# The matrices of the D transform loaded in eight transfers with the half as outer index, a new ranking of the first stage's work list, and the residual rows' first load in halves

## The chip, the cores and the metric

One core of a Trainium2 chip runs the whole program. The metric is the device time of one execution in microseconds, the median of several runs. The engines that matter are PE (TensorE, matmuls), DVE (VectorE), ACT (ScalarE), POOL (GpSimd) and SP (SyncE), which only issues transfers here. Transfers run on the core's 16 DMA engines.

## The reference

A transformer-like block on x of 2048 rows and 512 columns: a layer norm with a modulation from c, a Fourier mixing (a DFT over the 512 columns, then one over the 2048 rows, the real part kept), a residual, a second modulated norm, and a SwiGLU of width 1792. In float32, with tight agreement asked for.

```python
mod = (silu(c) @ w_mod).reshape(c.shape[0], 6, 1, -1)
sa, ca, ga, sb, cb, gb = (mod[:, i] for i in range(6))
h = layernorm(x) * (1 + ca) + sa
a = einsum("bsd,ed->bse", h, dft_hid_re)
b = einsum("bsd,ed->bse", h, dft_hid_im)
y = einsum("ts,bse->bte", dft_seq_re, a) - einsum("ts,bse->bte", dft_seq_im, b)
x = x + ga * y
h = layernorm(x) * (1 + cb) + sb
x = x + gb * ((silu(h @ w1) * (h @ w3)) @ w2)
```

## The kernel before

**Stages.** The first stage makes the D transform (over the 512 columns) of all 2048 rows, the second the sequence transform over the rows, the last the second norm and the SwiGLU. The stages follow each other on PE; transfers and preparations for a later one run beside an earlier one. The symmetry of the DFT matrices is used: rows s and 2048 - s are handled together, as sums and differences, which halves the matmuls. Sums of squares are formed beside the work to confirm that the matrices given have that symmetry; else a general path, which stands behind a branch, would compute all again.

**Precision.** Each float32 operand is split into a high and a low part; a product is three matmuls (high by high, high by low, low by high). ACT makes the high parts by a copy, DVE the low parts by a subtraction. So every matrix and every block passes ACT and DVE before PE can use it.

**The first stage.** The rows come in 8 blocks k of 256 (two sides of 128: a block and its mirror image). For each block: DVE takes the statistics of both sides (`stats`), ACT the root, DVE the inverse; ACT or DVE scale the two sides (`scale`, L468 or L470); PE transposes them (`turn`, L485); ACT or DVE apply the modulation (`mod`, L501 or L503, tile hm); DVE makes sums and differences (`sum`, tile hs); ACT their high parts (`hh`), DVE their low parts (`hl`); ACT also copies the mirror side (`h1`). PE then multiplies by the four D matrices dt = 0 to 3 (`prod`, L559), by their differences (`diff`, L576) and the mirror side (`mirror`, L598). ACT and DVE split the results into us, ul and uh, the operands of the sequence matmuls (L750). For block 4 the mirror part h1 has a low part too (DVE, tile h).

**The D matrices.** `load_hid(dt)` (L226 to L231) fetches one of four matrices into the tile raw_w[dt] (named w in the profile): 128 partitions, real and imaginary part side by side, 512 columns each. Partition q * 64 + r holds half q, row r of 64; in memory the rows r lie 8 KB apart and the two halves q 2 KB apart. Four transfers of 64 rows of 2 KB fetch one matrix. `w_highs` (ACT) and `w_lows` (DVE) split it into the tile wu, `w_minus` (ACT) makes a negated copy wn of the first two, `differ_w` (DVE) the differences wd.

**Order of the loads.** SP issues, in this order: cc, one side of x0, part of w_mod's rows (wmr), w0, w1, x1, w2, w3, x2, x3 and then one side of x4 to x7. ACT issues the other side of x0 and two loads of wmr. POOL fetches the mirrored sides of x4 to x7 by an indirect transfer, each behind a difference wd (`load_x`, L202).

**Order of the work.** After a fixed opening (norm of block 0, the modulation's vectors, some warming matmuls of L281 that keep PE busy), a planner orders the first stage: `task(name, rank, needs, fn, engine = us)` lists a piece of work, `arrange` takes again and again, among the pieces whose needs are met earliest within a window, the one with the lowest rank, and writes it to its engine. Ranks are a base per block (PACE 7.39) plus an entry of the table RANK; assumed arrival times of the loads are given by `at(...)` (L1518 to L1523). The result is one fixed order for each engine, and the engines run it strictly in that order. While the planned PE time has gaps before the first products, the planner fills them with warming matmuls.

**The residual.** `load_xt(t)` (L798) fetches a quarter of the rows of x, transposed, into two tiles; it is issued at step k = 2 (and 5) of a sequence pass, and `residual` first uses it at the end of step 3 (and 7).

Of the kernel before, what the change touches and what calls it, by code (L numbers as in the profile page):

```python
# [42 lines left out]
def folded(nc, pools, c, cp, wmr, wmc, x, xt, ctr, cti, wdr, wdi, w1, w3, w2, out):  # L43
# [15 lines left out]
    def take(dt=F32, what="s"):  # L59
        slot = free.popleft()  # L60
        count[0] += 1
        t = big.tile([P, 2, N], dt, name=f"{what}_{count[0]}", tag=f"slot{slot}")
        slot_of[id(t)] = (slot, t)
        return t
# [85 lines left out]
    mirror = consts.tile([P, NT, 2, NK // 2], I32, name="mirror")  # L150
# [73 lines left out]
    raw_w = {}  # L224

    def load_hid(dt, queue):  # L226
        i, par = HD[dt]
        raw_w[dt] = take(F32, "w")
        for m, w in enumerate((wdr, wdi)):
            for q in range(2):  # L230
                queue.dma_start(raw_w[dt][q * 64 : (q + 1) * 64, m, :], w[i][par::2, q])  # L231

    nc.sync.dma_start(cc, cp)
    load_x(0, nc.scalar)
# [4 lines left out]
    for dt in range(2):  # L239
        load_hid(dt, nc.sync)  # L240
    load_x(1)
    for dt in range(2, ND):
        load_hid(dt, nc.sync)
# [220 lines left out]
    def norm_scale(k, side, engine):  # L464
        r = rs[k][1]
        a, by, add = xz[k][:, side, :], r[:, 0, side : side + 1], r[:, 1, side : side + 1]
        if engine == "ACT":
            nc.scalar.activation(a, a, AF.Identity, bias=add, scale=by)  # L468
        else:
            nc.vector.tensor_scalar(a, a, by, add, op0=OP.mult, op1=OP.add)  # L470


    turned, hm, hs, h1 = {}, {}, {}, {}
    hh, hl = {}, {}
# [19 lines left out]
    def modulate_rows(k, dt, engine):  # L494
        if k not in hm:
            hm[k] = take(F32, "hm")
        src = turned[k][dt // 2][:, (dt % 2) * HALF : (dt % 2 + 1) * HALF]
        dst = four(hm[k])[:, dt, :]
        sa, ca1 = mod1[:, 0, dt : dt + 1], mod1[:, 1, dt : dt + 1]
        if engine == "ACT":  # L500
            nc.scalar.activation(dst, src, AF.Identity, bias=sa, scale=ca1)  # L501
        else:
            nc.vector.tensor_scalar(dst, src, ca1, sa, op0=OP.mult, op1=OP.add)  # L503
# [35 lines left out]
    uh, us, ul = {}, {}, {}  # L539
# [256 lines left out]
    xr = {}  # L796

    def load_xt(t):  # L798
        xr[t] = [take(F32, "xr") for _ in range(2)]
        for i in range(2):  # L800
            nc.sync.dma_start(xr[t][i], xt[t, i])

    def residual(t, e, src, gate):
        xs = xr[t][e // 2][:, e % 2, :]
# [261 lines left out]
    turn = [0, 0]  # L1066
# [393 lines left out]
    def at(us, *names):  # L1460
        for name in names:
            ends[name] = (us, "DMA")

    def last_steps(k):
# [6 lines left out]

    PACE = 7.39
    RANK = {
        "stats": -18.2,
        "root": -47.5,
        "inverse": -47.1,
        "scale": -41.6,
        "turn": -4.3,
        "mod": -3.8,
        "sum": -42.2,  # L1480
        "hh": -19.0,
        "hl": -6.5,
        "h1": -11.0,
        "prod": 2.1,
        "odd": -9.0,
        "mirror": 61.7,
        "uh": 12.4,
        "us": 4.0,
        "ul": 3.9,
        "diff": 21.3,  # L1490
        "up": -6.8,
        "ush": 27.9,
        "ulh": 31.5,
    }
    seq_steps = []
    keep_warm(3)
# [21 lines left out]
    at(10.0, "turn0.0", "turn0.1")  # L1518
    for dt in range(ND):
        at(13.6 + 0.25 * dt, f"modc{dt}")  # L1520
        at((13.4, 15.2, 18.3, 20.3)[dt], f"w{dt}")
    for k in range(1, 4):
        at((16.5, 21.8, 23.3)[k - 1], f"x{k}")  # L1523
    clear.update(PE=14.2, DVE=14.5, ACT=12.2, POOL=9.0, SP=9.0)
    for k in range(4, NK):
        task(f"load{k}", 2 * k - 7, [f"wd{min(k - 4, 2) + 1}"], lambda k=k: load_x(k), POOL=1.0)
# [10 lines left out]
    for k in range(NK):  # L1537
        r = k * PACE
        both = [f"{k}.0", f"{k}.1"]
        if k:  # L1540
# [10 lines left out]
            for s in range(2):  # L1551
                task(
                    f"scale{k}.{s}", r + RANK["scale"] + s, [f"inverse{k}"],
                    lambda e, k=k, s=s: norm_scale(k, s, e), ACT=0.71, DVE=0.46,
# [5 lines left out]
        for dt in range(ND):  # L1560
            task(
                f"mod{k}.{dt}", r + RANK["mod"] + 0.1 * dt, [f"modc{dt}", *[f"turn{n}" for n in both]],
                lambda e, k=k, dt=dt: modulate_rows(k, dt, e), ACT=0.45, DVE=0.46,
# [83 lines left out]
    for n, (j, k) in enumerate(steps):  # L1647
        if k == 2:
            load_xt(j + 2)
        if k == 5:  # L1650
            load_xt(j)
# [884 lines left out]
def fnet_swiglu_block(  # L2536
# [26 lines left out]
    pools = consts, small, big, psum  # L2563
    args = c, cp, wmr, wmc, x, xt, ctr, cti, wdr, wdi, w1, w3, w2, out
    bad = folded(nc, (*pools, dram, tc), *args)
    flag = nc.values_load(
        bad[0:1, 0:1],
# [62 lines left out]
```

## Time and profile before

| | |
|---|---|
| median of 3 runs (lowest, highest) | 692.43 us (691.5, 692.43) |
| the profiled execution: its own time | 691.3 us |
| its span in the profile | 689.5 us |
| granted clock of PE | 0.997 |
| DMA: packets, MB, mean rate | 40262, 116.80 MB, 169 GB/s |
| window 60 to 70 us: PE, DVE, ACT busy | 8.71, 9.48, 8.03 us |

The span begins with the first instruction of the program and ends with the last; the 1.8 us between it and the profiled time lie outside. In the profile's rows, "12.76 0.42 ACT L87 ..." is a start, a duration (both us), the engine, the line of the kernel, the operation and its operands; "[0.99 <-DMA w]" says that the engine was idle 0.99 us before it, and what ended that. A row of a table by windows gives the window, its length, each engine's busy time with its number of instructions, PE's granted clock, the busy share of the 16 DMA engines and the GB/s that they moved. SPq and POOLq are the queues from which these engines issue transfers. Buffer numbers are left out, so w stands for all four raw matrices.

### The profile page before, as it was taken

Reading aid. Unit: us, or ns where it says so; the run is one execution under the profiler, and the core shown is the slowest. Engines: PE = TensorE matmul, PEld = TensorE weight load, DVE = VectorE, ACT = ScalarE, POOL = GpSimd, SP = SyncE. Lnnn points to the kernel's source line nnn. Section 1 sums busy time; section 2 is a strip of 40 time slices with the busy share of each in tenths; the row PEclk is TensorE's granted clock in tenths of the full one; section 3 lists DMA queues with packets and bytes.
Section 4 is the critical chain, followed back from the end, with each engine's and each line's share of the span. In section 5 each row is a group of like instructions: output and inputs, shape, how many; then the busy total and the mean of one; then the engine's idle time right before and its main releaser. Section 6 shows DMA issues by size and latency. Waiting matters only on the chain.

```text
span 689.5 us, 9030 instructions
## 1 busy us (share of the span) xinstructions
PE 673.1 (98%) x3122; PEld 557.5 (81%) x3122; DVE 586.7 (85%) x945; ACT 451.2 (65%) x751; POOL 134.2 (19%) x156
## 2 busy tenths in 40 slices
PE   6999999999999999999999999999999999999996
PEld 4898788888888888888788888887878888888785
DVE  5999769997999977989997989787998979888375
ACT  4998956455343665663577767867677887877520
POOL 1320172544435000100101101011012112221100
PEclk9999999999999999999999999999999999999998
DMA  8730199887678441274757666466939998999813
GB/s 264 222 125 1 52 371 329 261 293 262 190 291 291 153 149 30 51 135 122 134 140 127 150 153 123 96 131 120 277 74 213 162 202 165 180 217 170 182 42 126
DMA packets 40262, 116.80 MB, mean 169 GB/s; under 512 B 5137, under 2 KB 5393, under 8 KB 40209
## 3 DMA queue, kind: packets, MB, share of 16 engines
q0 software_dynamic: 14512, 50.86, 36.8%
q1 hardware_dynamic: 25264, 63.98, 27.9%
q10 hardware_dynamic: 432, 1.31, 0.5%
q8 instruction: 26, 0.43, 0.3%
q14 instruction: 28, 0.22, 0.1%
HBM read 76.81 MB, written 41.42 MB: 171 GB/s over the span
## 4 chain that ended last, share of the span: by engine, by line
PE 75%; issue 8%; DVE 7%; ACT 4%; DMA 4%; POOL 1%; SPq 1%; POOLq 0%; DVEq 0%; ACTq 0%
PE bank L100 45%; PE bank L750 26%; DMA sum<-y 2%; PE bank L559 2%; POOL sum L1352 1%; PE bank L598 1%; DMA w<-in_wdr 1%; SPq L231 1%; DVE xr L805 1%; PE bank L576 1%; DMA x<-in_x 1%; ACT y L335 0%; DVE ul L90 0%; DVE hl L90 0%; ACT hh L87 0%
## 5 line engine op out<-in xcount | busy, mean ns | idle before, releaser
L100 PE MATMUL bank<-hf,w2h 128*128 128x512 f32 (+1 forms) x352 | 108.3, 389 | 0.0
L87 ACT ACTIVATE hf<-v 128x512 fp32r<-128x512 f32 x71 | 44.4, 631 | 67.3 <-DVE v L96 54.4
L335 ACT ACTIVATE y<-bank,gb 128x512 f32<-128x512 f32 x118 | 76.5, 682 | 4.0 <-PE bank L100 3.9
L100 PEld LDWEIGHTS bank<-hf,w2h 128*128 128x128 f32 x352 | 65.6, 188 | 15.3 <-ACT y L335 1.5
L1160 POOL DMA_DIRECT2D sum<-y x28 | 24.0, 857 | 240.7 <-ACT y L335 124.6
L100 PE MATMUL bank<-hf,w2l 128*128 128x512 f32 (+1 forms) x176 | 68.2, 387 | 0.0
L90 DVE TENSOR_TENSOR hf<-v,hf 128x512 fp32r<-128x512 f32 x71 | 48.7, 686 | 10.4 <-ACT hf L87 10.3
L1352 POOL DMA_DIRECT2D sum<-y x35 | 29.8, 852 | 128.8 <-ACT y L335 119.8
L87 ACT ACTIVATE x<-bank 128x512 f32<-128x512 f32 x72 | 41.8, 591 | 13.5 <-PE bank L100 12.6
L750 PE MATMUL bank<-l,us 128*128 128x512 f32 x128 | 49.9, 390 | 0.0
L750 PE MATMUL bank<-d,us 128*128 128x512 f32 x128 | 49.9, 390 | 0.0
L750 PE MATMUL bank<-bh,us 128*128 128x512 f32 x128 | 49.9, 390 | 0.0
L750 PE MATMUL bank<-d,uh 128*128 128x512 f32 x128 | 49.9, 390 | 0.0
L750 PE MATMUL bank<-bh,ul 128*128 128x512 f32 x128 | 49.8, 389 | 0.0
L750 PE MATMUL bank<-l,uh 128*128 128x512 f32 x128 | 49.8, 389 | 0.0
L170 POOL DMA_INDIRECT re<-in_ctr,mirror x32 | 36.3, 1136 | 65.5 <-ACT im L188 40.1
L170 POOL DMA_INDIRECT im<-in_cti,mirror x32 | 34.2, 1069 | 32.5 <-PE bank L750 8.5
L93 DVE TENSOR_TENSOR x<-bank,x 128x512 f32<-128x512 f32 x36 | 24.7, 685 | 17.8 <-PE bank L100 17.8
L100 PEld LDWEIGHTS bank<-hf,w2l 128*128 128x128 f32 x176 | 33.1, 188 | 6.7
L1244 ACT ACTIVATE v<-v 128x512 f32<-128x512 f32 x36 | 22.6, 629 | 23.2 <-DVE v L93 22.8
L93 DVE TENSOR_TENSOR v<-bank,x 128x512 f32<-128x512 f32 x36 | 24.7, 686 | 14.9 <-PE bank L100 14.0
L100 PE MATMUL bank<-h2h,w1h 128*128 128x512 f32 x80 | 31.2, 390 | 0.0
(260 smaller groups left out, 1902.1 us busy)
## 6 DMA issues: line engine op xcount, KB each, us to landing
sum<-y POOLq DMA_DIRECT2D x63, 512.0 KB, 5.5
w<-in_w SPq DMA_DIRECT2D x42, 512.0 KB, 5.0
re<-in_ctr SPq DMA_DIRECT2D x32, 256.0 KB, 5.4
im<-in_cti SPq DMA_DIRECT2D x32, 256.0 KB, 5.2
wmc<-in_wmc SPq DMA_DIRECT2D x8, 512.0 KB, 7.9
xr<-in_xt SPq DMA_DIRECT2D x8, 512.0 KB, 8.0
sum<-xr SPq DMA_DIRECT2D x8, 512.0 KB, 6.3
x<-in_x SPq DMA_DIRECT2D x11, 256.0 KB, 4.6
```

Source lines behind the costliest of these rows:

```text
L87: nc.scalar.activation(dst, src, AF.Copy, scale=scale)
L90: nc.vector.tensor_tensor(out=dst, in0=a, in1=b, op=OP.subtract)
L93: nc.vector.tensor_tensor(out=dst, in0=a, in1=b, op=OP.add)
L100: nc.tensor.matmul(acc, lhs[a], rhs[b], start=first and n == 0, stop=last and n == len(PASSES) - 1, skip_group_check=more,)
L170: nc.gpsimd.indirect_dma_start(dst, None, rows, bass.IndirectOffsetOnAxis(ap=at, axis=0))
L231: queue.dma_start(raw_w[dt][q * 64 : (q + 1) * 64, m, :], w[i][par::2, q])
L335: nc.scalar.activation(dst, src, AF.Identity, scale=by)
L559: nc.tensor.matmul(halves(hb[k])[:, m, :], sides((hh, hl)[a][k])[:, dt, m, :], wu[dt][:, b, m, :], start=False, stop=dt % 2 == 1 and n == ...
L750: nc.tensor.matmul(acc[what, e], lhs, rhs, start=begin and i == 0, stop=(end or (turn and what == "x")) and i == len(terms) - 1, skip_grou ...
L1160: nc.gpsimd.dma_start(sums[t, d // 2], y, accum_op=OP.add)
L1244: behind(k != 0 or q == 0, lambda: nc.scalar.activation(v, src, AF.Silu))
L1352: nc.gpsimd.dma_start(sums[t, which], y, accum_op=OP.add)
```

## The change

Three edits.

```diff
         for m, w in enumerate((wdr, wdi)):
-            for q in range(2):
-                queue.dma_start(raw_w[dt][q * 64 : (q + 1) * 64, m, :], w[i][par::2, q])
+            queue.dma_start(raw_w[dt][:, m, :], w[i][par::2].rearrange("r q n -> q r n"))
...
         xr[t] = [take(F32, "xr") for _ in range(2)]
-        for i in range(2):
-            nc.sync.dma_start(xr[t][i], xt[t, i])
+        for q in range(2):
+            nc.sync.dma_start(xr[t][0][:, q, :], xt[t, 0, :, q])
+        nc.sync.dma_start(xr[t][1], xt[t, 1])
...
     RANK = {
-        "stats": -18.2,
-        "root": -47.5,
...
+        "stats": -18.7,
+        "root": -45.0,
...
     for dt in range(ND):
         at(13.6 + 0.25 * dt, f"modc{dt}")
-        at((13.4, 15.2, 18.3, 20.3)[dt], f"w{dt}")
+        at((12.4, 14.2, 17.2, 18.8)[dt], f"w{dt}")
     for k in range(1, 4):
-        at((16.5, 21.8, 23.3)[k - 1], f"x{k}")
+        at((15.8, 20.6, 22.3)[k - 1], f"x{k}")
```

A part (real or imaginary) of a D matrix is now one transfer of 128 rows of 2 KB, whose source counts the half q outermost (2), then the row r (64). The destination is the same. All twenty entries of RANK and the assumed arrivals of w0 to w3 and x1 to x3 have new values, so that the planner makes another order. The first of the two tiles of each residual load comes in two transfers of 256 KB.

On SP, in the opening, the loads of the first two matrices (w) and of block 1 (x). Before:

```order
L231 DMA w_99<-in_wdr 64x512 x2
L231 DMA w_99<-in_wdi 64x512 x2
L231 DMA w_104<-in_wdr 64x512 x2
L231 DMA w_104<-in_wdi 64x512 x2
L209 DMA x_109<-in_x 128x1x512
```

Now:

```order
L230 DMA w_99<-in_wdr 128x1x512
L230 DMA w_99<-in_wdi 128x1x512
L230 DMA w_102<-in_wdr 128x1x512
L230 DMA w_102<-in_wdi 128x1x512
L209 DMA x_105<-in_x 128x1x512
```

Half the rows, in the same places of the queue; the other two matrices follow x1 in the same way.

On ACT, around the conversion of the last two matrices (wu from w_112 and w_117 before, from w_108 and w_111 now; wn is a negated copy, rs the root of block 1, hh and h parts of block 0, x the scaling of block 1, hm its modulation). Before:

```order
L87 ACTIVATE wn_244<-wu_224 128x1024
L454 ACTIVATE rs_235<-mv_234,eps 128x2
L87 ACTIVATE wu_250<-w_112 128x256 x2
L87 ACTIVATE hh_255<-hs_246 128x4x128
L468 ACTIVATE x_109<-x_109,rs_235 128x512
L87 ACTIVATE wu_294<-w_117 128x256 x2
L87 ACTIVATE hh_255<-hs_246 128x4x128
L87 ACTIVATE h_35_308<-hm_219 128x512
L501 ACTIVATE hm_314<-bank_31_288,mod_147 128x256 x2
```

Now:

```order
L87 ACTIVATE wu_233<-w_108 128x256 x2
L453 ACTIVATE rs_224<-mv_223,eps 128x2
L87 ACTIVATE hh_240<-hs_236 128x4x128
L87 ACTIVATE wu_244<-w_111 128x256 x2
L87 ACTIVATE h_30_273<-hm_211 128x512
L87 ACTIVATE hh_240<-hs_236 128x4x128
L467 ACTIVATE x_105<-x_105,rs_224 128x512
L87 ACTIVATE wn_295<-wu_213 128x1024
L500 ACTIVATE hm_307<-bank_32_289,mod_139 128x256 x2
```

The scaling of x1 and the second negated copy wn have moved from ahead of the last matrix's conversion to behind it.

On DVE, around the scaling of block 5 (x_380 before, x_385 now; hs, h and hl are parts of block 4, ho is the odd half of block 3). Before:

```order
L93 TENSOR_TENSOR hs_627<-hm_597 128x4x128
L90 TENSOR_TENSOR hs_627<-hm_597 128x4x128
L459 RECIPROCAL rs_537<-rs_537 128x2
L460 SCALAR_TENSOR_TENSOR rs_537<-mv_536,rs_537 128x2
L470 TENSOR_SCALAR x_380<-x_380,rs_537 128x512 x2
L93 TENSOR_TENSOR ho_549<-bank_70_508,ho_549 128x512
L90 TENSOR_TENSOR h_90_662<-hm_597,h_90_662 128x512
L90 TENSOR_TENSOR hl_673<-hs_627,hh_646 128x1024
```

Now:

```order
L93 TENSOR_TENSOR hs_627<-hm_591 128x4x128
L90 TENSOR_TENSOR hs_627<-hm_591 128x4x128
L458 RECIPROCAL rs_599<-rs_599 128x2
L459 SCALAR_TENSOR_TENSOR rs_599<-mv_598,rs_599 128x2
L90 TENSOR_TENSOR h_89_648<-hm_591,h_89_648 128x512
L93 TENSOR_TENSOR ho_532<-bank_71_513,ho_532 128x512
L469 TENSOR_SCALAR x_385<-x_385,rs_599 128x512 x2
L90 TENSOR_TENSOR hl_668<-hs_627,hh_652 128x1024
```

The scaling of x5 stands behind h and ho, no longer ahead of them.

More of the change, by code (lines that the diff above doesn't have):

```diff
@@ L1473, in folded @@
     RANK = {
-        "stats": -18.2,
-        "root": -47.5,
[L1476 to L1493, printed above, removed]
+        "stats": -18.7,
+        "root": -45.0,
+        "inverse": -61.3,
+        "scale": -16.6,
+        "turn": -8.5,
+        "mod": -4.5,
+        "sum": -74.2,
+        "hh": -16.7,
+        "hl": -4.4,
+        "h1": -22.1,
+        "prod": 4.2,
+        "odd": -82.1,
+        "mirror": 90.1,
+        "uh": 21.2,
+        "us": 25.0,
+        "ul": 0.6,
+        "diff": 18.2,
+        "up": -0.8,
+        "ush": 21.0,
+        "ulh": 47.4,
     }
```

## The prediction

> **What bounds the kernel now.** I read the page first, then PE's waits in the first stage, then the loads in front of that stage.
>
> ```profile
> span 689.5 us, 9030 instructions
> ...
> PE 673.1 (98%) x3122; PEld 557.5 (81%) x3122; DVE 586.7 (85%) x945; ACT 451.2 (65%) x751; POOL 134.2 (19%) x156
> ...
> PE 75%; issue 8%; DVE 7%; ACT 4%; DMA 4%; POOL 1%; SPq 1%; POOLq 0%; DVEq 0%; ACTq 0%
> ```
>
> PE is busy for 98% of the span, and three quarters of the chain of waits are PE's own work. What the change touches lies before the first sequence matmul. Some of PE's work there is only the warming matmuls of L281, so 98% tells nothing of that part. From the first product on, PE waits like this (waits by engine and line, then the timeline):
>
> ```profile
> PE bank L549 <- DVE ho L93: 1.8, 2, 1.6
> PE bank L598 <- ACT h L87: 1.0, 1, 1.0
> PE bank L559 <- ACT hh L87: 0.4, 1, 0.4
> PE bank L100 <- ACT y L335: 0.5, 1, 0.5
> PE bank L100 <- ACT x L87: 0.4, 1, 0.4
> ...
> 21.87 0.51 PE L559 MATMUL bank<-wu,hh 128*128 128x256 f32 x2 [0.44 <-ACT hh L87]
> ...
> 83.76 0.39 PE L750 MATMUL bank<-bh,us 128*128 128x512 f32 x1
> ```
>
> The first product starts at 21.87 us, the first sequence matmul at 83.76, with 3.2 us of waits between (L549, L598, L559; the two of L100, 0.9 us, belong to the last stage). That 3.2 us is all that a better order behind the loads could return; an earlier start comes on top. What sets 21.87? These rows of ACT and of the matrices' transfers:
>
> ```profile
> 12.76 0.42 ACT L87 ACTIVATE wu<-w 128x256 fp32r<-128x256 f32 x1 [0.99 <-DMA w<-in_wdr]
> ...
> 17.30 1.23 SPq L231 DMA_DIRECT2D w<-in_wdi  x2
> ...
> L231 SPq DMA_DIRECT2D w<-in_wdr x8: 465/596/618, 4.2 to 16.7; - x8
> ...
> 19.45 1.05 ACT L87 ACTIVATE wn<-wu 128x1024 fp32r<-128x1024 f32 x1
> ...
> 21.72 0.81 ACT L468 ACTIVATE x<-x,rs 128x512 f32<-128x512 f32 x1
> 22.43 0.71 ACT L87 ACTIVATE wu<-w 128x256 fp32r<-128x256 f32 x2
> ...
> DMA to landing us min/median/max: 3.5/4.5/7.9
> ```
>
> ACT has all four matrices to convert, in a fixed order. The last piece is issued at 17.9 us (second of the two at 17.30), with the median of 4.5 us it is there at about 22.4, and the conversion of the last matrix (ACT, 22.43) follows at once. From that conversion to the first sequence matmul are 83.76 - 22.43 = 61.33 us. Whatever moves the last matrix moves the whole rest one for one, unless another wait comes first.
>
> **The change part by part.** *The transfers.* The number of bytes is the same, in 8 issues in place of 16. SP saves 8 x 0.6 = 4.8 us of issuing (596 ns each in the row above). What matters is how fast one transfer runs. The rates, by stretch (last two columns: share of the 16 DMA engines, GB/s):
>
> ```profile
> 5.00:10.00 5.00, 3.18 (x12) 1.58 (x11) 2.76 (x8) 2.23 (x5) 0.00 (x0) 1.00 1.03 408
> 10.00:15.00 5.00, 3.91 (x28) 3.04 (x27) 4.24 (x7) 2.60 (x5) 0.00 (x0) 1.00 1.08 256
> 15.00:17.00 2.00, 2.00 (x20) 2.00 (x19) 1.11 (x7) 0.92 (x3) 0.00 (x0) 1.00 0.97 308
> 26.00:28.00 2.00, 2.00 (x15) 1.66 (x13) 1.94 (x4) 2.00 (x4) 1.83 (x2) 1.00 0.97 343
> ```
>
> One busy engine moves 408/16/1.03 = 24.8 GB/s (5 to 10 us, partly rows of 4 KB), 16 (the old w transfers of 64 rows, 10 to 15 us, taken as full), 19.8 and 22.1 (15 to 17 and 26 to 28 us, x rows of 2 KB). All that is with 16 engines. Does the new transfer use 16? Its source now counts 2 (the half), then 64 rows; every transfer of before counts 64 or 128 rows first. How these were shared out can be read off ACT's queue:
>
> ```profile
> q1 hardware_dynamic: 25264, 63.98, 27.9%
> q10 hardware_dynamic: 432, 1.31, 0.5%
> ...
> wmr<-in_wmr ACTq DMA_DIRECT2D x2, 512.0 KB, 6.8
> ...
> x<-in_x ACTq DMA_DIRECT2D x1, 256.0 KB, 3.5
> ```
>
> ACT issued three transfers of 128 rows, 384 packets; the other 48 of the 432 are 16 for each, an end mark from every engine. Rows counted by 64 x 2 (x) and by 128 (wmr) both went to all 16 engines, in equal shares of the outermost count (4 and 8). A share that is a run of the outermost loop is the simplest reading of both; with an outermost count of 2 there are only two shares, and 14 engines stand idle for each of the eight. No row of before has an outermost count under 64, so this is an inference and not a reading.
>
> The Trainium skill speaks to just this: "DMA: Bandwidth & Descriptors", section "Why a DMA increments its semaphore by 16 and not by 1", says that a transfer runs on the largest number of engines, up to 16, that divides the slowest count (other than 1) of both its sides, and its "Rules for kernel authors" warn of an outermost count below 16. By it the number here is 2, and the sum is the one that follows; the transfers of before, with 64 and 128, agree with it, and no run here shows a smaller one.
>
> On two engines each carries half of 8 x 256 KB, 1049 KB. At 24.8 GB/s that takes 42.3 us, at 22.1 47.5, at 16 65.5. I take 23.6 (44.4 us): two engines alone have nobody to contend with, so the two fastest rows are nearest. x1's two halves stand between the matrices in the same queue, with 16 KB each per engine: 1.4 us more. The first: ACT's row at 12.76 starts when the first 256 KB are there, which at 256 GB/s take 1.0 us, so they flow in from about 11.7. The last piece then lands at 11.7 + 44.4 + 1.4 = 57.5 us in place of 22.4.
>
> *The list.* On ACT two rows change sides around the last conversion: x1's scaling and the second negation (wn) stood ahead of it and now stand behind it. Starts in the rows above give their cost: 22.43 - 21.72 = 0.71 and 20.40 - 19.45 = 0.95 (the statistics' root follows at 20.40). Of the last matrix's own two copies the first no longer waits for the second's transfer (-0.3 of the 0.71). So 61.33 + 0.71 + 0.95 - 0.3 = 62.7 us lie behind the landing. Queued on ACT behind this conversion, and so waiting with it, are the copy h of block 0, the high halves hh that PE's products need, and block 1's modulation; DVE's lows and PE wait for those. The rows for this and for DVE's part:
>
> ```profile
> 20.40 0.29 ACT L454 ACTIVATE rs<-mv,eps 128x2 f32<-128x2 f32 x1
> ...
> 47.98 1.00 DVE L470 TENSOR_SCALAR x<-x,rs 128x512 f32<-128x512 f32 x2
> 48.89 0.68 DVE L93 TENSOR_TENSOR ho<-bank,ho 128x512 f32<-128x512 f32 x1
> 49.68 0.69 DVE L90 TENSOR_TENSOR h<-hm,h 128x512 fp32r<-128x512 f32 x1
> ```
>
> On DVE x5's two scalings (47.98) stood ahead of h and ho and now stand behind both, 1.2 to 1.4 us later for PE's transposes; PE's waits of 3.2 us may go in exchange. I enter 0 for this pair, with bounds -3.2 and +1.4.
>
> *x2 to x7* queue behind the last matrix: two 256 KB transfers for x2 add 2 x 0.7 = 1.4 us, so it is there at 58.9. Before, x2 was first used about 2 us behind the last conversion; no further wait. POOL's mirrored x loads follow DVE's differences of these matrices and move with them.
>
> *The residual's first load* in two issues: four more on SP, 0.6 us each, and the same bytes. A load takes
>
> ```profile
> xr<-in_xt SPq DMA_DIRECT2D x8, 512.0 KB, 8.0
> ...
> 83.99 0.39 PE L750 MATMUL bank<-bh,ul 128*128 128x512 f32 x1
> ```
>
> 8.0 us, and is issued two steps ahead of its use. A step has 48 matmuls of L750, 0.23 us apart (83.76 and 83.99 for the first two), so the cover is 22 us: nothing, and with that cover gone 0.6 us each.
>
> **Sum.** First sequence matmul at 57.5 + 62.7 = 120.2, against 83.76: +36.4. Behind it PE has only the 0.9 us of waits at L100, none of them on a load, so all of it arrives at the end. The profiled execution took 691.3 us (span 689.5): 727.7. The median of the runs shown, 692.43, is 1.1 above it: 728.8, so 729.
>
> A sentence aside: the Trainium skill's "TensorE: Matmul & The Clock Gate", section "What's actually happening", has PE fall to half clock after some 3.4 us of idleness and rise after as much work; by that page my estimate is another 1 to 2 us when PE starts again, and no row of before has such a pause.
>
> **The rivals.**
>
> *Sixteen engines after all, no change.* For it: 64 x 2 was also a count over two loops, and went to 16. Against: its outer loop alone sufficed. The new transfer would then take what x's does, 256 KB at 308 GB/s = 0.85 us. Ten transfers stand up to the last matrix (w0, w1, x1, w2, w3): 11.7 + 8.5 = 20.2, 2.2 us ahead of now. The list takes 1.4 back (62.7 for 61.33): -0.8, or +0.6 with x5's 1.4: 691.6 to 693.0, within what can be told.
>
> *Sixteen engines and a better list, faster.* The same -0.8, and all the 3.2 us of waits gone: 688.4. Against it: the list moves x5 the other way, and DVE (third pair of the rows) has hardly a gap in which to catch up, so that waits mostly change their place:
>
> ```profile
> 40.00:50.00 10.00, 10.00 (x76) 9.56 (x75) 9.69 (x22) 9.53 (x20) 1.21 (x2) 1.00 0.46 153
> 50.00:60.00 10.00, 10.00 (x69) 9.25 (x68) 9.81 (x20) 9.38 (x20) 0.00 (x0) 1.00 0.01 2
> ```
>
>
> *Sixteen engines, slower by little.* The new transfers run no faster than the old (16 GB/s per engine, 1.0 us for 256 KB): last matrix 11.7 + 8 x 1.0 + 2 x 0.85 = 21.4, -1.0, +1.4 of list, +1.4 of x5, and one more wait of that kind: 694 to 696. It decides once the last matrix lands later than about 21, where the earlier start no longer pays for the list.
>
> **How the numbers follow.** Two engines 0.80: both kinds of transfer that the rows show are consistent with shares of the outermost count, and neither needs another rule. The unchanged case 0.09, faster 0.06, slower by little 0.05. The bound to tell a difference from none is about 0.2%, 1.4 us. Faster 0.06, same 0.09, slower 0.85. The likeliest case's own range: 24.8 GB/s gives 42.3, 2.1 us less, with the 3.2 us of waits gone 723.5, and 720 if the two engines gain as much again without neighbours; 19.8 GB/s gives 53.0, 8.6 us more, with x5's 1.4 and x3 to x7 late by their own 4 x 0.7 us 742. I give 720 to 742; it leaves out the cases near 692 (0.20) and a little of the tail at 16 GB/s (21 us more, 750).
>
> **What would show it.** On two engines: the small packets of q1 fall (8 x 2 end marks in place of 16 x 16), so that with the residual's 4 x 144 extra packets q1 counts 25264 - 240 + 576 = 25600, against 25712 with sixteen; between 12 and 57 us the DMA runs near 47 GB/s; the time from issue to landing of w goes up to some 35 us; ACT's conversions start at about 17 to 22, 33, 45 and 57; PE's first sequence matmul comes at about 120, and the rest is the old length. Wrong: w landing by 20 to 22 us, PE's first product near 21, q1 at 25712. A last matrix at 57 with an end near 692 would say that the chain behind it is not one for one.

## The result and the profile after

| | before | after |
|---|---|---|
| median (6 runs each) | 692.43 us | 731.17 us |
| lowest, highest | 691.5, 693.07 | 730.35, 732.27 |
| ratio, 95% interval | | 1.0556, 1.0543 to 1.057 |
| the profiled execution, its span | 691.3, 689.5 us | 731.64, 729.8 us |

The change costs 38.7 us. First the page of the changed kernel: its span, the busy time of the engines, the chain that ended last, and the packets of the queues.

```profile
span 729.8 us, 9020 instructions
PE 678.6 (93%) x3122; PEld 561.4 (77%) x3122; DVE 588.5 (81%) x948; ACT 451.0 (62%) x748; POOL 134.3 (18%) x156
...
q1 hardware_dynamic: 25600, 63.98, 25.8%
...
PE 71%; issue 6%; DMA 6%; DVE 6%; SPq 4%; ACT 4%; POOL 1%; POOLq 0%; ACTq 0%; DVEq 0%
```

PE does the same 3122 matmuls. Its busy time grew by 5.5 us, while the span grew by 40.3: PE stands idle. q1 counts 25600 packets, the number that the prediction gave for two engines (25712 stood for sixteen).

Next ACT's timeline (start, duration, engine, line, operands; in brackets the idle time ahead and what ended it). Each row converts one half of a matrix, the real or the imaginary part:

```profile
16.13 0.42 ACT L87 ACTIVATE wu<-w 128x256 fp32r<-128x256 f32 x1 [4.11 <-DMA w<-in_wdr]
21.40 0.42 ACT L87 ACTIVATE wu<-w 128x256 fp32r<-128x256 f32 x1 [4.85 <-DMA w<-in_wdi]
...
50.01 0.42 ACT L87 ACTIVATE wu<-w 128x256 fp32r<-128x256 f32 x1 [4.79 <-DMA w<-in_wdr]
55.91 0.42 ACT L87 ACTIVATE wu<-w 128x256 fp32r<-128x256 f32 x1 [5.48 <-DMA w<-in_wdi]
```

Every conversion waits 4 to 5.5 us for its own transfer. The first two are 5.27 us apart: 262,144 bytes in that time are 49.7 GB/s, 24.9 GB/s for each of two engines. PE's rows and waits (waits by engine and line: total, times, longest) show where that arrives:

```profile
PE bank L558 <- ACT hh L87: 33.2, 2, 24.4
PE bank L484 <- DVE x L469: 1.3, 1, 1.3
PE bank L558 <- ACT ho L87: 0.7, 1, 0.7
```

```profile
57.42 0.79 PE L558 MATMUL bank<-wu,hh 128*128 128x256 f32 x2 [8.79 <-ACT hh L87]
...
121.41 0.39 PE L749 MATMUL bank<-bh,us 128*128 128x512 f32 x1
```

PE waits 33.2 us for ACT's high halves hh, which stand behind the late conversions in ACT's queue. The first sequence matmul (L749 now) comes at 121.41 in place of 83.76. The windows table has the window, its length, PE's busy time with its number of instructions, then those of the other engines, the granted clock, the share of the 16 DMA engines and GB/s. Two stretches of the loads show the two engines directly, since a share of 0.13 is two of sixteen:

```profile
15.00:20.00 5.00, 5.00 (x47) 5.00 (x46) 0.69 (x5) 0.42 (x1) 0.00 (x0) 1.00 0.13 50
...
30.00:40.00 10.00, 0.00 (x0) 0.00 (x0) 3.26 (x7) 3.14 (x6) 0.00 (x0) 0.50 0.13 50
```

Two more stretches are needed for the rest. Behind them stand SP's closing waits of both kernels (operation, number, durations, first and last start): of the kernel before, then of the changed one.

```profile
57.40:62.80 5.40, 5.38 (x21) 5.00 (x22) 3.74 (x9) 4.33 (x8) 0.00 (x0) 0.50 0.20 70
62.80:121.40 58.60, 55.98 (x372) 50.45 (x371) 54.30 (x105) 52.59 (x107) 11.54 (x14) 1.00 0.19 60
```

```profile
L2572 SPq EVENT_SEMAPHORE  x8: 17/17/17, 687.3 to 687.8; - x8
```

```profile
L2572 SPq EVENT_SEMAPHORE  x8: 17/17/17, 725.4 to 728.2; - x8
```

PE's clock is 0.50 for its first 5.4 us after the pause, so 2.7 us of work take twice their time. And SP's eight closing waits, 0.5 us before, take 2.8 us now. The sum, beside the prediction's:

| | predicted | measured |
|---|---|---|
| last conversion of a matrix | 57.5 | 55.91 |
| from there to the first sequence matmul | 62.7 | 65.50 |
| first sequence matmul | 120.2 | 121.41 |
| from there to the end of the execution | 607.5 | 610.2 |
| the profiled execution | 727.7 | 731.6 |

### The profile page after: what moved, and what is told of

Read it like the earlier page. It is cut to its first block, busy times and chain, and to the rows that moved or that the text cites. A ratio compares the mean times of both kernels' runs of the same rounds, so it can differ in the third digit from the quotient of the medians.

```text
span 729.8 us, 9020 instructions
## 1 busy us (share of the span) xinstructions
PE 678.6 (93%) x3122; PEld 561.4 (77%) x3122; DVE 588.5 (81%) x948; ACT 451.0 (62%) x748; POOL 134.3 (18%) x156
## 3 DMA queue, kind: packets, MB, share of 16 engines
q1 hardware_dynamic: 25600, 63.98, 25.8%
## 4 chain that ended last, share of the span: by engine, by line
PE 71%; issue 6%; DMA 6%; DVE 6%; SPq 4%; ACT 4%; POOL 1%; POOLq 0%; ACTq 0%; DVEq 0%
PE bank L100 42%; PE bank L749 24%; SPq L230 3%; DMA w<-in_wdi 3%; DMA sum<-y 3%; PE bank L597 2%; PE bank L558 1%; POOL sum L1352 1%; SPq L209 1%; PE bank L484 1%; DMA x<-in_x 1%; DVE xr L805 1%; ACT y L334 0%; ACT uh L87 0%; PE bank L575 0%
## 5 line engine op out<-in xcount | busy, mean ns | idle before, releaser
L100 PE MATMUL bank<-hf,w2h 128*128 128x512 f32 (+1 forms) x352 | 108.3, 389 | 0.0
L100 PEld LDWEIGHTS bank<-hf,w2h 128*128 128x128 f32 x352 | 65.6, 188 | 15.3 <-ACT y L334 1.4
L100 PE MATMUL bank<-hf,w2l 128*128 128x512 f32 (+1 forms) x176 | 68.1, 387 | 0.0
L558 PE MATMUL bank<-wu,hh 128*128 128x256 f32 x128 | 25.1, 295 | 34.0 <-ACT hh L87 33.2
L749 PE MATMUL bank<-bh,us 128*128 128x512 f32 x128 | 49.9, 390 | 0.0
L749 PE MATMUL bank<-bh,ul 128*128 128x512 f32 x128 | 49.8, 389 | 0.0
L749 PE MATMUL bank<-d,us 128*128 128x512 f32 x128 | 49.8, 389 | 0.0
L749 PE MATMUL bank<-d,uh 128*128 128x512 f32 x128 | 49.8, 389 | 0.0
L749 PE MATMUL bank<-l,us 128*128 128x512 f32 x128 | 49.8, 389 | 0.0
L749 PE MATMUL bank<-l,uh 128*128 128x512 f32 x128 | 49.8, 389 | 0.0
L558 PEld LDWEIGHTS bank<-wu,hh 128*128 128x128 f32 x128 | 21.1, 198 | 35.6 <-ACT hh L87 33.7
L100 PEld LDWEIGHTS bank<-hf,w2l 128*128 128x128 f32 x176 | 33.1, 188 | 6.6
```

Of the source, the lines that this page charges most:

```text
L100: nc.tensor.matmul(acc, lhs[a], rhs[b], start=first and n == 0, stop=last and n == len(PASSES) - 1, skip_group_check=more,)
L558: nc.tensor.matmul(halves(hb[k])[:, m, :], sides((hh, hl)[a][k])[:, dt, m, :], wu[dt][:, b, m, :], start=False, stop=dt % 2 == 1 and n == ...
L749: nc.tensor.matmul(acc[what, e], lhs, rhs, start=begin and i == 0, stop=(end or (turn and what == "x")) and i == len(terms) - 1, skip_grou ...
```

## The experiments

Line numbers shift by a few between kernels; L558 and L559, L749 and L750 are the same lines.

### How many engines does a transfer get?

Four kernels keep the new list, the residual halves and eight transfers of 128 rows of 2 KB, and change only how the rows lie in memory and are counted. The host lays the D matrices out in another order; the general path's loads are fitted to it. With all rows in line the source is one run of 128 rows; with a = 2, 4 or 8 pieces, kept apart, the source counts a, then 128 / a.

```diff
-            queue.dma_start(raw_w[dt][:, m, :], w[i][par::2].rearrange("r q n -> q r n"))
+            queue.dma_start(raw_w[dt][:, m, :], w[i, par].rearrange("q r n -> (q r) n"))
...
     def hid(w):
-        return np.asarray(w).reshape(D, ND // 2, 2, P).transpose(1, 3, 2, 0)
+        w = np.asarray(w).reshape(D, ND // 2, 2, P // 2, 2)
+        return w.transpose(1, 4, 2, 3, 0)
```

That is all rows in line. Four pieces (2 and 8 alike):

```diff
-            queue.dma_start(raw_w[dt][:, m, :], w[i][par::2].rearrange("r q n -> q r n"))
+            queue.dma_start(raw_w[dt][:, m, :], w[i, :, par])
...
     def hid(w):
-        return np.asarray(w).reshape(D, ND // 2, 2, P).transpose(1, 3, 2, 0)
+        w = np.asarray(w).reshape(D, ND // 2, 4, 32, 2)
+        return w.transpose(1, 2, 4, 3, 0)
```

All rows in line:

> The changed kernel with each part of a matrix lying in one piece in memory (the rows of both halves in line), so that the same eight transfers of 256 KB count 128 rows outermost. By shares of the outermost count all 16 engines take part: 256 KB in about 0.85 us as for x, the last matrix there at about 20 to 21, PE's clock at full, time 691.5 to 693.5. If eight large transfers are slow whatever their count (each held up by its size or its target of 128 partitions): still near 729 to 731.

Two pieces:

> The changed kernel with the rows of each half in line in memory (64 rows of 2 KB in one piece), the two halves apart, so that the transfer still counts 2, then 64. If the outermost count sets the engines: two, parts of a matrix 5.2 us apart, q1 at 25600 packets, about 729 (the exit code's pause is gone as in the run with moved exit code). If the rows' distance of 8 KB in memory made the transfers slow: as with all rows in line, 693, q1 at 25712.

Four pieces:

> The same with four pieces of 32 rows, counting 4, then 32. If the outermost count sets the engines: four, parts 2.7 us apart, last conversion at about 34, time 704 to 709, q1 at 25616 packets. If a count under 16 always falls back to two engines (or one): 729 and more, 25600. If only a count of 2 is slow: 693.

Eight pieces:

> Pieces of 16 rows, counting 8, then 16. In the run with 4 pieces parts came about 2.7 us apart, half of the 5.3 with 2. If engines go with the outermost count: 1.35 us apart, a last conversion at about 23 to 24 us, q1 at 25648 packets, time 694 to 698 (a first product one or two us later than before's, the new list's 1 us). If 8 already gives the full rate: 693.

| outermost count | q1 packets | two parts apart, us | GB/s of an engine | last conversion | time |
|---|---|---|---|---|---|
| 2, rows 8 KB apart (the change) | 25600 | 5.27 | 24.9 | 55.91 | 731.17 |
| 2, rows in line | 25600 | 5.27 | 24.9 | 55.01 | 729.77 (one run) |
| 4, rows in line | 25616 | 2.64 | 24.8 | 36.62 | 710.94 (one run) |
| 8, rows in line | 25648 | 1.43 | 22.9 | 28.30 | 699.83 (one run) |
| 128, rows in line | 25712 | 0.69 | 23.7 | 20.88 | 693.29, ratio 1.0005 (0.9989 to 1.0021) |

The rows follow one rule: as many engines as the outermost count, up to 16, each at 23 to 25 GB/s, and one end mark fewer for each engine left out (8 transfers by 16 minus the count: 25712 - 112 = 25600, - 96 = 25616, - 64 = 25648). The counts run are all powers of two; what another count would give is not shown. Rows in line with a count of 2 are as slow as rows 8 KB apart, so the addresses are not the cause. In the last row of the table the first of the two conversions waited for nothing, so its 0.69 is a lower bound and 23.7 an upper one; that kernel's window of 10 to 15 us, 389 GB/s at a share of 1.05, gives 23.2 for an engine. ACT's rows of the kernels with four pieces and with eight, from which two parts' distance is read:

```profile
19.66 0.42 ACT L87 ACTIVATE wu<-w 128x256 fp32r<-128x256 f32 x1 [1.78 <-DMA w<-in_wdr]
22.30 0.42 ACT L87 ACTIVATE wu<-w 128x256 fp32r<-128x256 f32 x1 [2.22 <-DMA w<-in_wdi]
```

```profile
14.28 0.42 ACT L87 ACTIVATE wu<-w 128x256 fp32r<-128x256 f32 x1 [0.85 <-DMA w<-in_wdr]
15.71 0.42 ACT L87 ACTIVATE wu<-w 128x256 fp32r<-128x256 f32 x1 [1.01 <-DMA w<-in_wdi]
```

These are the shortest distances with 4 and with 8; for a count of 2 the table has the first two parts, and the shortest were 5.19 us (the change) and 5.04 (rows in line).

The times came out above what was expected for 4 and 8 (704 to 709 and 694 to 698): the parts behind x1 came 1.6 to 2.3 us apart with 8, and up to 4.0 with 4. In the changed kernel, too, the last two distances are 5.9 us. The windows of PE there (last four numbers: busy time and count, clock, DMA share, GB/s) show that rows of x moved beside them in part of that time:

```profile
52.00:54.00 2.00, 0.00 (x0) 0.67 0.77 229
54.00:56.00 2.00, 0.00 (x0) 0.50 0.13 50
```

Where the share is 0.13, from 27 to 32 and from 39 to 44 us, the parts are 5.2 to 5.3 us apart. So they come slower where x's rows move as well; that x's rows are the whole cause was not tested.

### What do the new list and the residual halves do by themselves?

The changed kernel with the sixteen transfers of before put back:

> The changed kernel with the matrices loaded in sixteen transfers of 64 rows again; the new list and the residual halves stay. If the whole loss lies in the transfers (two engines for each), the 36 us and the slow clock behind them go, and what is left is the list's own price: +1.4 us (62.7 for 61.33 us behind the last matrix), so 692.4 + 1.4 = 694, between 693 and 696 with one more wait in the first stage. If the list is a gain of its own, as PE's 3.2 us of waits would allow: 689 to 691. If a good part of the loss were the list's or the residual's: over 700.

Measured: 694.13, ratio 1.0012 (0.9997 to 1.0027): by the time as the first case said, and by the ratio 0.8 us of its 1.4, since the kernel before took 693.32 beside it. From its PE timeline:

```profile
21.03 0.74 PE L559 MATMUL bank<-wu,hh 128*128 128x256 f32 x4 [0.69 <-ACT hh L87]
...
84.76 0.40 PE L750 MATMUL bank<-bh,us 128*128 128x512 f32 x1
```

The list starts PE 0.84 us earlier (21.03 for 21.87) and has it at the sequence 1.00 us later (84.76 for 83.76). It costs 1 us in itself, within what can be told.

The kernel before with the eight new transfers alone (the first edit of the diff, nothing else):

> The kernel before with the eight new transfers alone; old list, residual in whole tiles. If the transfers make the loss and the list hardly counts: last conversion of a matrix at about 56, then the old list's 61.3 us and 2.7 us more for PE's half clock, first sequence matmul at about 120, 728.5 to 730.5. SP's closing waits stand six places earlier than in the changed kernel's code, so if their pause is a code fetch it comes after about seven of them, and is some 0.4 us shorter. If the loss needs the new list (an order that fits late matrices badly): under 720.

Measured: 728.05, ratio 1.0515 (1.0494 to 1.0536), half a microsecond under the expected range; last conversion at 55.51, first sequence matmul at 118.69. So the transfers alone make 36 of the 38.7 us, 1.7 of them by a pause at the program's end (below). From the last conversion to the sequence are 63.18 us, for 65.50 in the changed kernel and 61.33 before; PE's clock is at half in both late kernels, so 2.3 us of the 65.50 are the list's. The prediction had 0.71 + 0.95 = 1.66 for it; the 0.3 that it took off is the conversion's own and belongs to both late kernels. By the same reckoning the late matrices with PE's half clock cost the old list 63.18 - (61.33 - 0.3) = 2.15 us.

The residual's halves alone:

> The kernel before with the residual's first tile loaded in halves alone; loads of the matrices and list as before. If the four more issues lie in the 22 us between a load's issue and its use: no change, ratio 0.999 to 1.001, PE's waits behind the first sequence matmul 0.9 us as before, q1 at 25264 + 576 = 25840 packets. If they held up other loads in SP's queue: up to 4 x 0.6 = 2.4 us more.

Measured: 692.19, ratio 0.9993 (0.9977 to 1.0009), 25840 packets in q1; PE's waits at L100, which are on ACT, were 1.9 us for 0.9. They cost nothing that can be told.

### Fast loads with the old list, and with one of their own

The kernel before with all rows in line and one transfer for a part. The unused general path loads its matrices in more pieces.

> The kernel before (old list, residual in whole tiles) with each part of a matrix in one piece in memory and loaded in one transfer of 128 rows. The last matrix lands 1 to 2 us earlier than in the kernel before. If the list can use it, 690 to 691.5; if ACT's fixed order behind the loads (the second negation, x1's scaling) sets the first product, no change: 691.8 to 693. Beside the run with the new list it gives the list's worth under fast loads.

Measured: 692.48, ratio 0.9988 (0.9973 to 1.0002): no change that can be told. By its completion events the last matrix was there at 17.88 us, for 22.00 in the kernel before: four microseconds earlier, and nothing came of it. The windows show the rate (last column), ACT's timeline why:

```profile
10.00:15.00 5.00, 3.91 (x28) 3.04 (x27) 4.24 (x7) 2.59 (x5) 0.00 (x0) 1.00 1.05 388
```

```profile
16.08 1.02 ACT L500 ACTIVATE hm<-bank,mod 128x256 f32<-128x256 f32 x2 [3.20 <-DVE mod L323]
16.99 0.72 ACT L87 ACTIVATE wu<-w 128x256 fp32r<-128x256 f32 x2
17.61 1.05 ACT L87 ACTIVATE wn<-wu 128x1024 fp32r<-128x1024 f32 x1
...
22.43 0.72 ACT L87 ACTIVATE wu<-w 128x256 fp32r<-128x256 f32 x2
```

388 GB/s for 256, and yet from 16.08 on ACT's rows are those of the kernel before, to the hundredth of a microsecond. ACT stands 3.20 us until DVE has the modulation's vectors, and from then it is busy without a gap until it reaches the last matrix at 22.43. The same rows of the kernel before read the same way:

```profile
16.08 1.02 ACT L501 ACTIVATE hm<-bank,mod 128x256 f32<-128x256 f32 x2 [1.92 <-DVE mod L324]
16.99 0.71 ACT L87 ACTIVATE wu<-w 128x256 fp32r<-128x256 f32 x2
```

So a last matrix at 22.00 was early enough to be covered: the opening was set by the modulation's vectors and ACT's work behind them, not by the loads.

A list ranked for the fast loads (same kernel, other numbers in the table and in the assumed arrivals, here the latter):

```diff
-        at((13.4, 15.2, 18.3, 20.3)[dt], f"w{dt}")
+        at((11.3, 13.6, 14.7, 19.4)[dt], f"w{dt}")
...
-        at((16.5, 21.8, 23.3)[k - 1], f"x{k}")
+        at((15.7, 17.4, 22.0)[k - 1], f"x{k}")
```

> The kernel before with all rows of a matrix part in line (one transfer of 128 rows on 16 engines) and a list ranked for these arrivals (eighteen numbers of the table and the assumed arrivals changed; the last matrix's conversion stands behind the high halves of block 0 and x1's scaling, the second negation stays ahead). With the old list these loads brought the last matrix 4 us earlier and PE's first sequence matmul not at all (83.77). If ACT's order was what held it, the first sequence matmul comes at 82.4 to 83 and the time is 690.8 to 691.8, ratio 0.997 to 0.999. If DVE, busy 93% of that stage, holds it whatever ACT does: 83.5 to 84, ratio 0.999 to 1.001.

Measured: 691.77, ratio 0.9984 (0.9972 to 0.9995), a gain of 1.1 us (by the medians 0.8) that is just clear of no change and smaller than the 0.2% that one can rely on. The time fits the first case, but its profile does not show the reason that this case gave: the execution profiled was the slowest of the twelve (694.13; lowest 689.85), and its first sequence matmul comes at 85.43, not at 82.4 to 83. The windows of PE (last four numbers: busy time and count, clock, DMA share, GB/s) show one difference:

```profile
10.00:16.00 6.00, 5.56 (x19) 0.50 1.05 390
```

In that execution PE runs at half clock from about 10 to 16 us; in the profiled execution before the clock was 1.00 there. PE's first product is at 24.06. That this half clock makes the slow end of these twelve runs is a guess that was not tested, and whether ACT's order or DVE held the sequence back stays open.

### PE's clock

The changed kernel, its planner told of the late arrivals, so that it puts warming matmuls in the gaps:

```diff
-        at((12.4, 14.2, 17.2, 18.8)[dt], f"w{dt}")
+        at((21.3, 32.1, 44.0, 55.8)[dt], f"w{dt}")
...
-        at((15.8, 20.6, 22.3)[k - 1], f"x{k}")
+        at((33.3, 57.8, 58.4)[k - 1], f"x{k}")
```

> The changed kernel, its planner told the arrivals that the changed kernel's trace shows (21.3, 32.1, 44.0, 55.8 for the matrices, 33.3 for x1, 57.8 and 58.4 for x2 and x3). The planner then fills PE's gaps with warming matmuls, up to the last matrix. If 2.7 us of the loss are PE's half clock from 57.4 to 62.8, they go: PE's clock 1.0 from 57 on, 727 to 729 with the exit code's pause as in the changed kernel. If the clock costs nothing on the way to the end (another engine sets it): 731. The loads stay the bound, so no time under 722.

Measured: 747.81, ratio 1.0811 (1.0786 to 1.0835). It missed by 20 us, for a reason that DVE's waits and its timeline tell:

```profile
DVE st L448 <- DMA x<-in_x: 18.2, 1, 18.2
```

```profile
61.70 0.69 DVE L448 BATCH_NORM_STATS2 st<-x 128x6 f32<-128x512 f32 x1 [18.18 <-DMA x<-in_x]
...
63.32 0.39 DVE L90 TENSOR_TENSOR wu<-w,wu 128x256 fp32r<-128x256 f32 x1
```

DVE stood 18.2 us for rows of x with the third matrix's low parts behind them in its queue. The planner takes x4 for present 6 us after POOL's issue, about 41 us; SP's half of it waits in the queue behind the matrices. With a limit for x4 to x7 as well (`at(55.0 + k, f"side{k}")` as one more need of each):

> The changed kernel with the planner told when things arrive, x4 to x7 too. In the run before, told of the matrices and x1 to x3 alone, it took x4's rows (which SP's queue holds behind the matrices) for present at about 41 us, and set x4's statistics on DVE ahead of the third matrix's low parts: DVE stood 18.2 us there. With that mended the matrices' low parts stand ahead of all late rows, and PE's gaps are filled with warming matmuls. If 2.7 us of the loss are PE's half clock from 57.4 to 62.8: clock 1.0 there, 725 to 729 (less if products of block 1 done ahead of the last matrix shorten the rest too). If the clock is paid by nobody: 731.

Measured: 726.53, ratio 1.0488 (1.0462 to 1.0515), clock 1.00 from 20 us on:

```profile
57.00:64.00 7.00, 7.00 (x54) 6.48 (x53) 4.88 (x14) 4.33 (x10) 0.00 (x0) 1.00 0.24 78
```

Its first sequence matmul is at 117.72, 59.2 us behind the last conversion (58.50) for 65.50. The 6.3 us are the clock and the products done ahead together; this run doesn't part them. Nor is the time's whole gain on the changed kernel (4.6 us) of that kind: this kernel has no second pause at the program's end (below), and the changed kernel without that pause took 728.74, so 2.2 us are left, with a last conversion 2.6 us later. That the half clock costs up to 2.7 us by itself rests on the windows shown above (5.4 us at 0.50); the 2.15 us of the run with the transfers alone agree with most of it being paid.

### The end of the program

Behind DVE's last instruction the changed kernel takes 2.65 us longer to its end (8.65 for 6.0). The kernel with four more loads in the general path, which is never run:

```diff
-            if key not in first:
+            if key[0] in ("wr", "wi"):
+                for q in range(2):
+                    nc.sync.dma_start(raw[key][:, q], source[key][0][:, q])
+            elif key not in first:
                 nc.sync.dma_start(raw[key], source[key][0])
```

> The changed kernel with four more load instructions for SP in the general path, which stands behind a branch and is never run: only the place of the program's closing instructions moves, by four. The changed kernel's end was 2.65 us longer behind the last work of DVE than before's (8.65 for 6.0), with 2.3 us of it SP standing still between two of its closing waits, after the first two of eight. If that is the fetch of the next piece of code, the pause goes and the time falls by 2.3 us: 731.2 to about 729, ratio to before 1.052 to 1.053. If the pause is a wait for a late transfer, or has to do with the late loads: no change, 1.0555.

Measured: 728.74, ratio 1.0509 (1.0487 to 1.053), 2.4 us less than the changed kernel, by the place of instructions alone. SP's pauses there by the table of waits (total, times, longest; changed kernel first, then this one), and this one's eight closing waits:

```profile
SPq L2572 <- SPq L2572: 5.0, 2, 2.7
```

```profile
SPq L2575 <- SPq L2575: 2.7, 1, 2.7
```

```profile
L2575 SPq EVENT_SEMAPHORE  x8: 17/17/17, 724.2 to 724.8; - x8
```

Two pauses became one, and behind DVE's last instruction its end takes 6.2 us for 8.65. The place of the closing instructions decides, counted as SP's instructions ahead of them in the program:

| kernel | place | second pause after | of |
|---|---|---|---|
| new transfers alone | 585 | 7 instructions | 1.69 us |
| the change | 590 | 2 | 2.25 us |
| true arrivals, first try | 591 | 1 | 2.27 us |
| before | 593 | none | |
| the ten others | 594 to 618 | none | |

All three point to a border at 592, and the kernel with the transfers alone had been expected to pause after about seven (five places ahead of the changed kernel, not the six of its text). The simplest reading is a fetch of code: ahead of the border the branch over the general path brings a piece of code of which only 7, 2 or 1 instructions are of use, and the next must be fetched too. The runs show the place and the pauses; that they are fetches is argued. The Trainium skill, "Runtime: NRT & Kernel Launch", section "Instruction fetch mechanics", says that code comes in blocks and that a taken branch to a place not held forces a fetch; the pause of 2.5 to 2.8 us that every kernel here has behind the branch agrees. The place of the border and the second pause are from these runs alone.

## Why the prediction was right

The forecast was 729 us, 720 to 742; measured were 731.17. The mechanism was the forecast one. That the sum came so near is partly luck, as its terms missed by 1.6, 2.8 and 2.7 us and the first with the other sign.

**Two engines.** Right, and now shown: the count of packets, the share of 0.13, the parts 5.27 us apart, and the ladder of counts 2, 4, 8, 128. The rule of the Trainium skill that the prediction weighed ("DMA: Bandwidth & Descriptors", section "Why a DMA increments its semaphore by 16 and not by 1") gives all five rows of that table. The trace of before allowed this only as an inference, since it had no count under 64. Two of the signs named for it missed: the mean rate from 12 to 57 us was 94 GB/s and not 47, as rows of x move in that time too, and the last part was converted 20.7 us behind the start of its issue (35.2 to 55.91) and not some 35 behind, since its issue itself came late (below).

**The rate.** Taken as 23.6 GB/s for an engine. The first two parts give 24.9, like the fastest row of before (24.8); from the first conversion to the last, less the 1.4 us for x1, a part takes (55.91 - 16.13 - 1.4) / 7 = 5.48 us, which is 23.9. The last matrix is there 1.6 us earlier than forecast (55.91 for 57.5): half of it is this rate, half an earlier begin (16.13 - 5.27 = 10.9 for 11.7).

**The list behind the last matrix.** The term of 62.7 us was too small by 2.8. The run with the transfers alone parts it: 2.15 us come with the late matrices whatever the list, and PE's half clock, left out of the sum and named beside it as 1 to 2 us, is their likely cause; 0.66 are the list's (2.32 for 1.66). The 0 entered for x5's pair can't be read off by itself, but PE's waits up to the sequence are 3.1 us with the new list and the old loads, 1.3 of them at its transposes behind DVE's scaling, where there were none before, and were 3.2 before: they changed their place, as the prediction said. The Trainium skill's page "TensorE: Matmul & The Clock Gate" speaks in "What's actually happening" of a window of about 3.4 us that runs freely; 5.4 us at half clock (57.4 to 62.8) and 5.6 in the kernel with the transfers alone are longer than one window and shorter than two, which a window that starts on its own allows.

**The end.** 2.65 us between DVE's last instruction and the end were not in the sum at all. 2.25 of them are the second pause, which comes from neither data nor engines but from the place of SP's exit code; another count of instructions would have spared it. Without these 2.65 us the forecast of 727.7 for the profiled execution would have been 1.3 us off, with the two misses ahead of it partly cancelling.

**SP.** "SP saves 8 x 0.6 = 4.8 us of issuing" was wrong, and the forecast did not suffer from it. The issues are fewer and longer: SP's rows of the changed kernel (the issues at L230: shortest, median and longest in ns, first and last start) are

```profile
L230 SPq DMA_DIRECT2D w<-in_wdr x4: 559/2804/5151, 4.7 to 30.0; - x4
L230 SPq DMA_DIRECT2D w<-in_wdi x4: 1924/4398/5344, 5.4 to 35.2; - x4
```

An issue takes up to 5.3 us, as long as a transfer: once some transfers are queued, SP stands in the next issue. Everything else in SP's queue waits with it, which is why x4's rows were late in the run above; the first issue of x1's rows behind the second matrix takes 7.28 us itself.

**What the loads had set before.** Here the prediction was wrong in its reading of the kernel before. It took ACT's conversion at 22.43 for one that waits for the transfer, since the median landing time put the transfer at 22.4 too. The row had no idle time ahead of it; the run with the last matrix at 17.88 and the same conversion at 22.43 shows that ACT's own work set it. "Whatever moves the last matrix moves the whole rest one for one" holds for later, where the first wait to grow is the matrix, and not for earlier. The forecast did not suffer, since 33 us of delay pass any cover; the rivals with sixteen engines did. Their sum began with an end of 2.2 us ahead of now, and the loads in line give none of it (692.48).

**The rivals.** "Sixteen engines after all" is what the kernel with rows in line and the new list is: 693.29, ratio 1.0005, where that rival said 691.6 to 693.0 (1.0005 of 692.43 is 692.8). The better list as such was no gain (1.0012). **The residual** costs nothing, as said (0.9993).

## What to carry to other kernels

Before merging transfers, look at what each side counts outermost: here a count of 2 left 14 of 16 engines idle and cost more than all else in the change; rows laid in line give 388 GB/s for the same 128 rows. A load is worth speeding up only if the row that uses it shows idle time ahead of it; a row that follows its neighbour at once is held by its own engine, whatever the landing times say. And when a few microseconds at the end don't add up, look at the pauses behind the program's last branch, which go by the place of the code there, before suspecting the change.

## What the runs showed of the hardware that was not expected

- Four instructions that are never executed are worth 2.4 us (731.17 to 728.74), by the place of SP's exit code; the pause that goes is 2.25 us.
- Transfers on two engines hold the queue that issues them: once some are queued, 5.15 to 5.3 us in a single issue, for 0.33 to 0.6 us with sixteen, and 7.28 us in an issue of x's rows behind them.
- Sixteen transfers of 64 rows, 8 KB apart, move 256 to 284 GB/s, eight of 128 rows in line 388. Whether the number of rows or their distance makes this difference was not tried.
- PE's clock falls to half in the idle times of the late kernel, and from 57.42 on 5.4 us of work pass before it is full again. The 3.4 us of work from 45.27 on ran at 0.50 as well: the clock was 1.00 only behind them, from 50 to 52 us, when PE had nothing to do, and 0.50 again from 54. Warming matmuls up to the arrival (the second run with true arrivals) hold it at 1.00.
